# One 64x32 TensorE tile shape for attention scores and value products, and GpSimd copies of pairs of pairs

## The chip, the cores and the metric

The kernel runs on one core of one Trainium2 chip. The metric is the device time of one execution in microseconds; the number of a kernel is the median of its runs. TensorE is called PE, VectorE DVE, ScalarE ACT, GpSimd POOL, and SyncE, which starts most transfers, SP.

## What is computed

Two independent layers over 2048 positions of width 640, put side by side in the output (bf16):

```python
def _A_ref(x, Lambda_re, Lambda_im, B_re, B_im, C_re, C_im, log_dt, Dskip):
    dt = jnp.exp(log_dt)
    Lam_bar = jnp.exp(dt * Lam)                       # complex, one per state
    Bu = jnp.einsum("bld,pd->blp", x + 0j, B_bar)
    for t in range(L):
        h = Lam_bar[None, :] * h + Bu[:, t, :]
    y = 2.0 * jnp.einsum("blp,dp->bld", hseq, Cmat).real + x * Dskip[None, None, :]

def _B_ref(x, wq, wk, wv, wo):                        # 32 heads of 20, one key and one value head
    q = (x @ wq) ...                                  # [32 heads, 2048, 20]
    k = x @ wk
    v = x @ wv
    scores = jnp.einsum("bhqd,bkd->bhqk", q, k) * (Dh ** -0.5)
    p = _softmax(scores, axis=-1)
    return jnp.einsum("bhqk,bkd->bhqd", p, v) ... @ wo
```

A is a state-space layer, B an attention whose 32 heads share keys and values.

## The kernel before

**Attention, block by block.** A block is 512 queries of four heads; there are 4 x 8 = 32 of them. In each block the scores are made in 64 tiles of 128 keys by 512 queries of one head, so 2048 tiles in all (`NTILE`). A score tile is one product (`score`, L1616 to L1630): 32 rows of `KT` (20 of the head, one for a bias) by 128 keys as weights, 512 queries of `QT` moving. It fills a 32-row strip of the array (`tile_position=(32 * j, 0)`), and up to four of them, from four strips, run in one pass, each into a PSUM bank of its own.

**Two ways to the weights of the softmax.** Most tiles go through ACT: one exp of two or three banks (`fill`, L1530) into the ring `PR` of 24 slots. The others, called D tiles, go through DVE: a "first" (`fill_d`, recorded at L867) turns scores into an int16 whose bits read as a bf16 power of two, and three copies of it, shifted by 32, 64 and 96, are added up with weights of their own by the value product, which smooths the coarse exponential. A copy is an integer addition: on POOL two tiles at a time (`pool_source`, `copy`, L1858: `int64_add`), otherwise on DVE (`copy_source`). D tiles live in single slots of the tile `BIG`.

**Value products.** `pv_source` gathers one ready entry for each of the four heads; a product (`pv_fn`, L1946) has 128 keys by 32 columns of `VP` (or of `VS`, the values scaled for a shifted copy) as weights and 512 columns of weights moving, in a column strip (`tile_position=(0, 32 * j)`). All four accumulate in one PSUM bank (`MB`). A tile of ACT needs one such product and a D tile four. At the end of a block the bank is copied to `pvsb` (L1925) and the sums go through DRAM for their reciprocals.

**The other work.** Query projections, the output projection, and the state-space layer ("units", the C*B products, the y products) are tasks. Each takes a PSUM bank and puts its products in as PE has time (`ride`), four 32-column strips at a time (L800). Pieces of them, 32 rows at a time, also ride in a score pass that has a row strip free (`board`, `piece`, L810).

**The order of the work** is made by a planner in the kernel's own file (`Schedule`): engines take the steps that are ready by priority, with costs and due times written in as numbers (`STAGES` and others), some of them changing with the number of tiles begun. A step of PE has a mode, "S" for score passes and "C" for column strips, and changing it costs 97 ns in the plan. `port=True` marks steps of DVE and POOL which the plan never puts side by side. The order that comes out is emitted as one in-order instruction stream for each engine, with waits on semaphores (`Emitter`).

**PSUM** has eight banks: two groups of three for scores (`slots`), one for the value products, one for tasks (`misc`). The third bank of a group holds a third exp tile or a D tile of that pass.

Of the kernel before, what the change touches and what calls it, by code (L numbers as in the profile page):

```python
# [12 lines left out]
ALU = mybir.AluOpType  # L13
# [11 lines left out]
class Op:  # L25
# [3 lines left out]
                 "seq", "land", "dma_key", "idx", "tail", "mode", "load", "late", "port", "after", "due", "table", "psum", "twice", "rider", "fence", "lands", "clear")  # L29

    def __init__(self, eng, fns, dur, deps=(), prio=5, reads=(), writes=(), prev=None, gate=None, hook=None,
# [8 lines left out]
        self.twice = self.rider = None  # L40
# [6 lines left out]
class Schedule:  # L47
# [5 lines left out]
    ENGINES = ("pe", "act", "dve", "pool", "sp")  # L53
    OUT = {"pe": 200.0, "act": 130.0, "dve": 110.0, "pool": 150.0, "dma": 60.0}
    OWN = {"pe": 0.0, "act": 60.0, "dve": 115.0, "pool": 100.0}
# [3 lines left out]
    SLACK = {"pe": 60.0, "dve": 150.0}  # L59
# [50 lines left out]
    def seen(self, op, eng):  # L110

        if op.dma_key is not None:
            return op.end + self.OUT["dma"]
        if op.eng == eng:
            return op.end + self.OWN[eng] if eng in self.OWN else op.end
        return op.end + self.OUT[op.eng]

# [19 lines left out]
    def begin(self, op, eng):  # L137
# [5 lines left out]
        if eng == "pe":  # L143
            if op.mode != self.mode:
                op.dur += self.SWITCH
                self.mode = op.mode
            self.loads.append((self.t, op.load))
        if op.port:
# [25 lines left out]

    def pick(self, eng):
        urgent = None
        t = self.t
        cands = self.pending[eng]
# [26 lines left out]
        for op in can:  # L205
            p, dur = op.prio, op.dur
# [56 lines left out]
class Emitter:  # L263
# [9 lines left out]
    def plan(self):  # L273
        count = {e: 0 for e in Schedule.ENGINES}
        know = {e: {} for e in Schedule.ENGINES}
        snap = {}
# [4 lines left out]
        self.first = set()  # L281
        self.streams = {e: [] for e in Schedule.ENGINES}
        for op in self.order:
# [3 lines left out]
            def dep(o, key=None):  # L287
# [3 lines left out]
                if src == e and (e == "pe"):  # L291
                    return
                at = o.idx - 0.5 if key is not None and o.twice is not None and key != o.rider else o.idx
# [40 lines left out]
            for src, at, o in w:  # L334
# [4 lines left out]
                if at < o.idx:  # L339
                    self.first.add((id(op), id(o)))  # L340
# [17 lines left out]
        for e in ("pe", "act", "dve", "pool"):  # L358
            v = 0
            for op in self.streams[e]:  # L360
                if op.dma_key is None and id(op) in needed:
                    v += 1 if op.twice is None else 2
                    self.value[id(op)] = v
# [8 lines left out]
    def replay(self, rng):  # L372
# [3 lines left out]
        for op in self.order:  # L376
            e = op.eng
            t = free[e]
# [12 lines left out]
            else:  # L391
                end[id(op)] = t + op.dur + op.tail
                free[e] = t + op.dur - (S.EARLIER.get(e, 0.0) if op.psum else 0.0)
        return max(end.values())

    def emit(self, block):
        self.sems = {e: self.nc.alloc_semaphore(f"prog_{e}") for e in ("pe", "act", "dve", "pool")}
        self.dma_sems = {k: self.nc.alloc_semaphore(f"dma_{k}") for k in self.dma_keys}

        def run(e, be):  # L400
            for op in self.streams[e]:
                for o in self.waits_of[id(op)]:
                    if o.dma_key is not None:
                        be.wait_ge(self.dma_sems[o.dma_key], 16 * o.idx)
                    else:
                        be.wait_ge(self.sems[o.eng], self.value[id(o)] - ((id(op), id(o)) in self.first))
                ins = None
                for x, fn in enumerate(op.fns):
                    ins = fn(be)
                    if x == op.twice and id(op) in self.needed:  # L410
                        ins.then_inc(self.sems[e], 1)
                    if op.dma_key is not None:
                        ins.then_inc(self.dma_sems[op.dma_key], 16)
                if op.dma_key is None and id(op) in self.needed:
                    ins.then_inc(self.sems[e], 1)
# [23 lines left out]
class Ride:  # L439


    def __init__(self, bank, steps):
        self.bank, self.steps = bank, collections.deque(steps)
        self.open, self.last, self.end, self.rode = [], None, None, None
# [14 lines left out]
NQB, NKC, NGG = 4, 16, 8  # L459
NTILE = NQB * NGG * NKC * 4  # L460
# [7 lines left out]
class Build:  # L468
    CHUNKS = (3, 3)
    MISC = 1  # L470
    NPT = 24
    NOP = 7
    NRD = 3
    NDS = 20
    MORE = 21
# [71 lines left out]
    SPREAD = 18.658  # L547
    SEEDS, REPLAYS = (169732,), 12
# [28 lines left out]
    def quiet(self, order):  # L577
# [4 lines left out]
        for op in order:  # L582
            if op.eng == "pe":
# [3 lines left out]
        first = int(min(op.start for op in order if op.eng == "pe" and op.mode == "S") / step) - 20  # L587
        last = int(max(op.start for op in order if op.eng == "pe" and op.mode == "S") / step)
# [7 lines left out]
    def alloc(self, o):  # L596
# [27 lines left out]
        self.KT = sb(o, "KT", [128, S], BF16)  # L624
        self.VP = sb(o, "VP", [128, NKC, 32], BF16)
        self.VS = sb(o, "VS", [128, len(self.SHIFTS), NKC, 32], BF16)
# [6 lines left out]
        self.stg = sb(o, "stg", [128, 3, 512], BF16)  # L633
# [7 lines left out]
        self.lift = sb(o, "lift", [128, 4], FP32)  # L641
# [4 lines left out]
        self.dn = sb(o, "dn", [64, 2, 32], BF16)  # L646
        self.rc = sb(o, "rc", [64, 2, 32], BF16)
# [87 lines left out]
    GRAIN, KEEP_C = 256, 5  # L735

    def ride(self, bank, steps):

        p = self
        r = Ride(bank, [[list(m), list(deps), list(keys)] for m, deps, keys in steps])  # L740
        self.rides.append(r)

        def hook(op):
            mms, _, keys = r.steps[0]
            n = 0
            while mms and (not n or n + mms[0][2].shape[-1] <= p.GRAIN):
                out, lhsT, rhs = mms.pop(0)
                n += rhs.shape[-1]
                op.fns.append(p.product(r, out, lhsT, rhs, range(4), r.last is None))
                r.last = op  # L750
            op.reads = list(keys)
            if not mms:
                r.steps.popleft()
        while r.steps:
            mms, deps, keys = r.steps[0]
# [5 lines left out]
            op = self.pe([], self.mmt(n, k), deps=deps + (bank.last if r.last is None else []), prio=self.task_prio(), mode="C",  # L761
                         load=n, writes=[bank.key], hook=hook, gate=lambda: bool(r.steps))
            yield lambda: op.start is not None or not r.steps
            if op.start is None:
                self.s.pending["pe"].remove(op)
        while r.open:
            t0 = self.s.t
            self.s.at(t0 + self.PATIENCE)
            op = self.pe([], self.mmt(512), prio=1.5, mode="S", load=128.0, writes=[bank.key], hook=lambda op: self.alone(r, op),
                         gate=lambda: bool(r.open) and self.s.t >= t0 + self.PATIENCE - 1.0)  # L770
            yield lambda: op.start is not None or not r.open
            if op.start is None:
                self.s.pending["pe"].remove(op)
        self.rides.remove(r)
        return r.last

    PATIENCE = 2500.0

    def alone(self, r, op):

        step, left = r.open[0]
        x = min(left)
        left.remove(x)
        if not left:
            r.open.pop(0)
        op.fns = [self.piece(r, *m, x) for m in step[0]]
        op.reads = list(step[2])
        self.rode(r, op, x)
        self.n_alone += 1

    n_alone = 0

    def product(self, r, out, lhsT, rhs, cols, start):

        tag = object()
        r.end = tag
# [1876 lines left out]
```

## Time and profile before

| | us |
|---|---|
| runs: median (lowest to highest) of 3 | 697.88 (697.73 to 698.61) |
| profiled execution: span from first to last instruction | 695.9 |
| PE busy | 683.2 |
| ACT busy | 681.8 |
| DVE busy | 637.0 |
| POOL busy | 470.4 |

The profile's own time is its span; what lies around the span is in the runs only. The engine columns are the time in which at least one instruction of the engine was open. Products on PE are pipelined and their ends are modelled, so that a busy PE need not be at its peak; where the rhythm of PE matters, it is read from the starts of the products. `x` is a count of instructions; in the rows of groups, the number after the bar is busy time in all and the next the mean duration of one in ns, and behind the second bar stands the idle time of the engine just before them, with what ended it. In the rows of stretches the first pair is the stretch, then come the engines' busy times, the granted clock of PE as a share of the full one, the share of the DMA engines, and GB/s.

### The profile page before, as it was taken

To read this page: it belongs to the slowest core of one execution; us is meant where nothing else is said; L and a number is where in the kernel's file an instruction comes from. 1 tells how busy PE (TensorE), PEld (TensorE's weight loads), DVE (VectorE), ACT (ScalarE), POOL (GpSimd) and SP (SyncE) were. 2 spreads that over 40 slices of the span, in tenths; PEclk is the share of its full clock that TensorE was granted. 3 is DMA by queue.
4 is the path that set the end of the run, shared out by engine and by line. 5 is a ranking of instruction groups with operands and counts; after the bars stand their busy time and mean duration, and the time that the engine had idled before them with its cause. 6 is when DMAs were issued, how large, how long until landed. Compare 5 with 4: busy or idle time off the path is not lost.

```text
span 695.9 us, 27390 instructions
## 1 busy us (share of the span) xinstructions
PE 683.2 (98%) x11488; PEld 250.6 (36%) x11490; DVE 637.0 (92%) x1243; ACT 681.8 (98%) x703; POOL 470.4 (68%) x796
## 2 busy tenths in 40 slices
PE   8999999999999999999999999999999999999998
PEld 5322332334334333333433333334333332343335
DVE  7899999999999889999999999999999999977795
ACT  7999999999999999999999999999999999999996
POOL 4256666564587668767778777676776767788880
DMA  9659641211130111102110101131000001110001
GB/s 217 175 127 187 139 103 39 62 26 32 30 94 13 32 27 27 35 21 29 44 26 22 28 27 28 35 58 20 13 15 12 20 15 36 37 29 22 21 15 41
DMA packets 77591, 34.48 MB, mean 50 GB/s; under 512 B 58350, under 2 KB 77470, under 8 KB 77470
## 3 DMA queue, kind: packets, MB, share of 16 engines
q1 hardware_dynamic: 76650, 32.57, 20.3%
q8 instruction: 92, 1.51, 0.9%
q10 hardware_dynamic: 820, 0.16, 0.1%
q14 instruction: 29, 0.24, 0.1%
HBM read 11.53 MB, written 9.75 MB: 31 GB/s over the span
## 4 chain that ended last, share of the span: by engine, by line
PE 56%; ACT 42%; DVE 1%; issue 0%
ACT PR L1530 41%; PE MB L1946 21%; PE MB L800 14%; PE SC L1626 10%; PE MB L810 8%; PE MB L730 1%; DVE BIG L867 1%; PE SC L1162 1%; PE SC L726 1%; PE MB L726 0%; ACT L2197 0%; PE SC L730 0%; DVE pvsb L1925 0%; PE MB L1279 0%; DVE QT L867 0%
## 5 line engine op out<-in xcount | busy, mean ns | idle before, releaser
L1530 ACT ACTIVATE PR<-SC 128x1024 bf16<-128x1024 f32 (+1 forms) x678 | 666.6, 1131 | 4.5 <-PE SC L1626 3.3
L1858 POOL INT64_ADD BIG<-BIG x761 | 458.1, 617 | 198.1 <-DVE BIG L867 54.7
L867 DVE TENSOR_SCALAR BIG<-SC 128x512 int16<-128x512 f32 x560 | 376.2, 684 | 38.7 <-PE SC L1626 33.1
L1946 PE MATMUL MB<-BIG,VS 128*32 128x512 bf16 (+1 forms) x2468 | 269.8, 376 | 1.2 <-DVE pvsb L1925 0.9
L1626 PE MATMUL SC<-QT,KT 32*128 32x512 bf16 (+1 forms) x2073 | 265.3, 378 | 4.4 <-ACT PR L1530 1.8
L1946 PE MATMUL MB<-PR,VP 128*32 128x512 bf16 (+1 forms) x1495 | 222.3, 378 | 0.1
L1626 PEld LDWEIGHTS SC<-QT,KT 32*128 32x128 bf16 x2073 | 67.3, 91 | 133.8 <-ACT PR L1530 77.1
L1946 PEld LDWEIGHTS MB<-BIG,VS 128*32 128x32 bf16 x2468 | 68.5, 95 | 65.5 <-issue 41.4
L1946 PEld LDWEIGHTS MB<-PR,VP 128*32 128x32 bf16 x1495 | 55.1, 94 | 45.8 <-issue 33.0
L867 DVE TENSOR_SCALAR BIG<-BIG 128x1024 int16<-128x1024 int16 (+1 forms) x136 | 52.3, 419 | 0.9 <-PE MB L1946 0.4
L800 PE MATMUL MB<-CA,W 128*32 128x320 bf16 (+2 forms) x992 | 51.4, 299 | 0.4 <-DVE BIG L2366 0.4
L810 PE MATMUL MB<-xaT,BT 32*128 32x256 bf16 x192 | 37.1, 273 | 0.0
L800 PE MATMUL MB<-CT,W 128*32 128x512 bf16 (+1 forms) x640 | 36.0, 302 | 0.6 <-issue 0.6
L800 PE MATMUL MB<-xaT,BA 128*32 128x256 bf16 x800 | 31.8, 275 | 0.0
L810 PE MATMUL MB<-diagD,xaT 32*128 32x128 bf16 x320 | 31.3, 217 | 0.0
L810 PEld LDWEIGHTS MB<-diagD,xaT 32*128 32x128 bf16 x320 | 17.7, 92 | 29.1 <-ACT PR L1530 17.7
L800 PEld LDWEIGHTS MB<-CA,W 128*32 128x32 bf16 x992 | 22.8, 96 | 14.2 <-issue 5.7
L800 PE MATMUL MB<-xaT,BT 128*32 128x256 bf16 x608 | 26.2, 274 | 0.0
L2133 DVE CAST stg<-MB 128x512 bf16<-128x512 f32 x35 | 23.8, 680 | 1.8 <-PE MB L800 1.1
L862 DVE TENSOR_TENSOR prod<-MB,tab 128x1024 bf16<-128x1024 f32 x20 | 24.3, 1215 | 0.2
L867 DVE TENSOR_SCALAR BIG<-MB 128x512 int16<-128x512 f32 x35 | 23.8, 679 | 0.6 <-PE MB L1626 0.6
L2406 DVE TENSOR_TENSOR_SCAN g<-sc,hst,prod 128x256 bf16<-128x256 f32 x30 | 22.5, 749 | 0.0
(178 smaller groups left out, 502.4 us busy)
## 6 DMA issues: line engine op xcount, KB each, us to landing
out_dram<-stg SPq DMA_DIRECT2D x33, 128.0 KB, 2.0
qd<-BIG SPq DMA_DIRECT2D x20, 128.0 KB, 2.1
QT<-qd SPq DMA_DIRECT2D x28, 80.0 KB
OP<-pvsb SPq DMA_DIRECT2D x105, 20.0 KB
rdP<-recs SPq DMA_DIRECT2D x105, 20.0 KB
lbd<-BA SPq DMA_DIRECT2D x5, 320.0 KB, 2.7
CT<-in_B_x_dram SPq DMA_DIRECT2D x2, 640.0 KB, 5.3
BA<-in_A_B_re_dram SPq DMA_DIRECT2D x1, 800.0 KB, 7.5
```

The source lines that it names most:

```text
L726: r = e.matmul(out[32 * j:32 * j + 32], lhsT=lhsT[:, 32 * j:32 * j + 32], rhs=rhs, start=start, stop=stop, tile_position=(0, 32 * j), skip ...
L730: return lambda e: e.matmul(out, lhsT=lhsT, rhs=rhs, start=start, stop=stop, **kw)
L800: x = e.matmul(out[32 * j:32 * j + 32], lhsT=lhsT[:, 32 * j:32 * j + 32], rhs=rhs, start=start, stop=r.end is tag, tile_position=(0, 32 * ...
L810: return lambda e: e.matmul(out, lhsT=lhsT[at], rhs=rhs[at], start=start, stop=r.end is tag, tile_position=(32 * row, 0), skip_group_check ...
L862: return lambda e: e.tensor_tensor(out, a, b, op)
L867: return lambda e: e.tensor_scalar(out, a, s1, s2, op0=op0, op1=op1)
L1530: ex = self.act(lambda e: e.activation(dst, t[:, 0:512 * n], ACT.Exp, scale=1.0 / UNIT), 0.8333 * 512 * n + 64, table="exp", deps=[op], re ...
L1626: r = e.matmul(out[:, bank.off + lo:bank.off + lo + n], lhsT=p.KT[32 * j:32 * j + 32, 128 * c:128 * c + 128], rhs=p.QT[32 * j:32 * j + 32, ...
L1858: op.fns.append(lambda e: e.int64_add(words(dst), words(src), add))
L1946: r = e.matmul(bank.tensor[32 * j:32 * j + 32, bank.off + at:bank.off + at + n], lhsT=v[:, c, 0:32], rhs=rhs[:, lo:lo + n], start=first an ...
L2133: ev = self.dve(lambda e: e.tensor_copy(st, bank.ap), 645, deps=[prev], reads=[bank.key], writes=[key], prio=self.EV, gate=(lambda: last.e ...
L2406: o = self.dve(lambda e, ri=ri, init=init: e.tensor_tensor_scan(p.g[:, u, ri, :], rdec, p.prod[:, 1, 0, ri, :], init, ALU.mult, ALU.add), ...
```

## The change

**Scores.** A score tile now holds 64 keys by 512 queries for two heads, one in partitions 0 to 63 and one in 64 to 127. It takes four products of 64 rows by 32 columns, on one diagonal of the array's quadrants: rows 64 to 127 with columns 0 to 63, and rows 0 to 63 with columns 64 to 127 (`rows_at(1, j)`). The 64 rows hold two heads; `KT` is kept twice, each time with zeros in the rows of the other head. There are still 2048 tiles.

**Value products.** An entry is two products of 64 rows by 32 columns (`pv_add`), and two entries fill the other diagonal: rows and columns 0 to 63, rows and columns 64 to 127. D tiles need four entries as before.

**PE in the plan.** There are two lanes beside "pe", both in PE's one stream: "pt" for value products, "pb" for scores, each with half of the array. All of attention is one mode "U". The other work goes through both lanes, one lane after the other for each bank (`ride_source`); the rides in score passes (`board`, `piece`) are gone. A wait of one lane for a step of the other is a semaphore.

**D tiles.** They are taken singly by `d_source` whenever a bank is free, never as a part of a fill. The third banks of the two groups are shared by D tiles, tasks (`task_banks`) and third exp tiles. D tiles are held in pairs (`Pair`). POOL, or DVE, does copy 1 of a pair as one step of two tiles, and then copies 2 and 3 as one step of four tiles, which adds 64 to the first and to copy 1 (`step_of`, `CHAIN`). Copies by pairs need neighbouring slots.

**Sizes and numbers.** `PR` has 18 slots instead of 24; D slots 18 + 20 instead of 20 + 21; output staging 2 instead of 3; the cap on the share of D tiles (`SHARE`) 0.34 and 0.348 instead of 0.281 to 0.301. The first fill waits for the keys that it reads, not for all keys. The diagonal of the skip term of even rows is added into the C*B matrix once (`skip`) and leaves the y products. Reciprocals work on 128 x 16 instead of 64 x 32. There are new settings for the planner throughout, and functions to put state-space steps on POOL (`put`, `ON_POOL`), which the empty `ON_POOL` leaves unused.

The core of the diff:

```diff
-        self.KT = sb(o, "KT", [128, S], BF16)
-        self.VP = sb(o, "VP", [128, NKC, 32], BF16)
+        self.KT = sb(o, "KT", [128, 2, S], BF16)
+        self.VP = sb(o, "VP", [128, NHC, 32], BF16)
...
+    def rows_at(h, j):
+
+        t = h ^ j // 2
+        return slice(64 * t, 64 * t + 64), 64 * t
...
+    def ride_source(self, lane):
+
+        s = self.s
+        other = Schedule.HALVES[lane == "pt"]
+        for r in self.rides:
+            if not r.todo[lane] or r.on and lane not in r.on and r.todo[other]:
+                continue
+            o = r.on.get(other)
+            if o is not None and s.seen(o, lane) > s.t:
+                continue
...
-    def score(self, op, m, out, bank):
+    def scores(self, op, m, out, bank, deps=()):
...
-                r = e.matmul(out[:, bank.off + lo:bank.off + lo + n], lhsT=p.KT[32 * j:32 * j + 32, 128 * c:128 * c + 128],
-                             rhs=p.QT[32 * j:32 * j + 32, b % 12, at:at + n], start=True, stop=True, tile_position=(32 * j, 0))
+            for lo, c, q0, n in parts:
+                for j in range(4):
+                    at, row = self.rows_at(1, j)
+                    k = 64 * c + 32 * (j % 2)
+                    r = e.matmul(out[32 * j:32 * j + 32, bank.off + lo:bank.off + lo + n], lhsT=p.KT[at, x, k:k + 32],
+                                 rhs=p.QT[at, b % 12, q0:q0 + n], start=True, stop=True, tile_position=(row, 32 * j), skip_group_check=True)
...
+    def task_banks(self):
+
+        own = [b for b in self.free_banks if b in self.misc]
+        if not own and self.in_use < self.TASKS:
+            own = [b for b in self.free_banks if b in self.thirds]
+        return own
...
+    def step_of(self, d, free, eng):
+
+        s = self.s
+        if d.first is not None and len(d.todo) == 2 and len(d.tiles) == 2 and self.CHAIN:
+            if d.first[1].end is None or s.seen(d.first[1], eng) > s.t:
+                return None
+            if free > 1 and not self.short(d, 4):
+                return (2, 3)
+        if free < 1 or self.short(d, len(d.tiles)):
+            return None
+        return (d.todo[0],)
...
-        return Op("pool", [], self.POOL2, prio=1, port=True, hook=lambda op: self.copy(op, k, two, True))
-
-    POOL2 = 605.0
+        return Op("pool", [], self.POOL2 if len(ks) == 1 else self.POOL4, prio=1, port=True, hook=lambda op: self.copy(op, d, ks))
+
+    POOL2, POOL4 = 605.0, 1035.0
...
-    def pv_fn(self, b, j, v, kc, rhs, first, last):
+    def pv_add(self, op, b, j, entry, first, last):
...
+                for t in range(2):
+                    rows, to = slice(64 * t, 64 * t + 64), 32 * (2 * t + j)
+                    r = e.matmul(bank.tensor[to:to + 32, bank.off + at:bank.off + at + n], lhsT=v[rows, c, 0:32], rhs=rhs[rows, lo:lo + n],
+                                 start=first and not i, stop=last and i == len(parts) - 1, tile_position=(64 * t, to), skip_group_check=True)
```

More of the change, by code (lines that the diff above doesn't have):

```diff
@@ L733, in quads, with ride @@
         return self.QUADS and self.started
[L735 to L740, printed above, removed]
+    GRAIN = 256
+    def ride(self, bank, steps, cols=range(4)):
+        r = Ride(bank, steps, cols)
         self.rides.append(r)
[L743 to L755, printed above, removed]
+        yield lambda: not any(r.todo.values())
+        self.rides.remove(r)
+        return r.last
+    def ride_source(self, lane):
[7 more added lines that the diff above has]
+                continue
+            if r.last is None and any(o.end is None or s.seen(o, lane) > s.t for o in r.bank.last):
+                continue
+            mms, deps, keys = r.todo[lane][0]
+            if any(o.end is None or s.seen(o, lane) > s.t for o in deps):
+                continue
             n, k = 0, 0
@@ L774, in ride @@
[L774 to L796, printed above, removed]
+            return Op(lane, [], max(self.mmt(n, k), 32.0 * k), deps=list(r.bank.last) if r.last is None else (), mode="U", load=n / 2.0,
+                      prio=self.TASK2 if lane == "pt" else self.task_prio(), reads=keys, writes=[r.bank.key],
+                      hook=lambda op, r=r, k=k: self.ride_step(op, r, k))
@@ L1799, in copy_source @@
[L1799 to L1807 removed]
+        d, ks = can[0]
+        closing = d.b == self.pv_b and self.pv_filled[self.pv_b] == self.pv_need[self.pv_b]
```

905 lines of the change are left out of this document (454 added, 451 removed).

## The prediction

> **What bounds the kernel now.** I read the page's head first, then busy time by stretch, then groups by shape, then the waits and pieces of the timeline.
>
> ```profile
> span 695.9 us, 27390 instructions
> PE 683.2 (98%) x11488; PEld 250.6 (36%) x11490; DVE 637.0 (92%) x1243; ACT 681.8 (98%) x703; POOL 470.4 (68%) x796
> ```
> ```profile
> core 0: us, PE busy (x) PEld busy (x) DVE busy (x) ACT busy (x) POOL busy (x), PEclk, DMA share, GB/s
> 0.00:100.00 100.00, 96.49 (x1220) 34.31 (x1226) 91.18 (x234) 94.61 (x104) 54.34 (x105) 1.00 0.73 163
> 100.00:660.00 560.00, 554.35 (x9521) 200.31 (x9519) 518.93 (x956) 557.73 (x569) 399.45 (x664) 1.00 0.13 31
> 660.00:696.00 36.00, 32.34 (x755) 16.02 (x751) 26.92 (x55) 29.47 (x32) 16.61 (x28) 1.00 0.10 27
> ...
> 400.00:600.00 200.00, 197.17 (x3247) 68.38 (x3243) 194.02 (x362) 199.23 (x207) 145.09 (x244) 1.00 0.11 26
> ```
>
> Three engines look full; the clock is granted whole (1.00). ACT is truly full: 557.7 of 560 us in the middle. DVE has 518.9 of 560 there (92.7%), but 97.0% in the stretch 400 to 600. POOL has room.
>
> ```profile
> 18.41 1.02 ACT L1530 ACTIVATE PR<-SC 128x1024 bf16<-128x1024 f32 x1 [1.81 <-PE SC L1626]
> 682.14 5.54 ACT L1530 ACTIVATE PR<-SC 128x1024 bf16<-128x1024 f32 x5 [0.39 <-PE SC L1626]
> ```
> ```profile
> L1530 ACT ACTIVATE PR<-SC 128x1024 bf16<-128x1024 f32 (+1 forms) x678 | 666.6, 1131 | 4.5 <-PE SC L1626 3.3 <-PE MB L1626 0.3 <-PE MB L1946 0.2
> L867 DVE TENSOR_SCALAR BIG<-BIG 128x1024 int16<-128x1024 int16 (+1 forms) x136 | 52.3, 419 | 0.9 <-PE MB L1946 0.4
> ```
> ```profile
> L1530 ACT ACTIVATE PR<-SC 128x1024 bf16<-128x1024 f32 x579 | 544.7, 1068 | 4.3 <-PE SC L1626 3.3 <-PE MB L1626 0.3 <-PE MB L1946 0.2
> L1858 POOL INT64_ADD BIG<-BIG x761 | 458.1, 617 | 198.1 <-DVE BIG L867 54.7 <-PE MB L1946 22.1 <-DVE g L2406 19.3
> L867 DVE TENSOR_SCALAR BIG<-SC 128x512 int16<-128x512 f32 x560 | 376.2, 684 | 38.7 <-PE SC L1626 33.1
> L1530 ACT ACTIVATE PR<-SC 128x1536 bf16<-128x1536 f32 x98 | 141.6, 1505 | 0.1
> L867 DVE TENSOR_SCALAR BIG<-MB 128x512 int16<-128x512 f32 x35 | 23.8, 679 | 0.6 <-PE MB L1626 0.6
> ```
>
> So the work is 2048 score tiles of 128x512, each turned into weights either by ACT's exp or by DVE (a "first", then three shifted copies). DVE's are 560 + 35 = 595. The other 1453 are ACT's, 666.6 / 1453 = 0.459 us each. Exps begin at 18.41 and end at 682.14 + 5.54 = 687.7. So the span is 666.6 us of exps plus 29.3 of start, gaps and tail: **the span falls by 0.459 us for every tile that DVE takes from ACT.** A first costs DVE (376.2 + 23.8) / 595 = 0.672 us. DVE's copies are 52.3 us; everything else on DVE is 637.0 - 400.0 - 52.3 = 184.7. What keeps DVE from taking more is in its waits: 38.7 us before firsts, 33.1 of them for the score product on PE. Why it waits shows late in the kernel and in PE's rhythm:
>
> ```profile
> 626.32 0.69 DVE L867 TENSOR_SCALAR BIG<-SC 128x512 int16<-128x512 f32 x1 [0.18 <-PE SC L1626]
> 627.19 0.69 DVE L867 TENSOR_SCALAR BIG<-SC 128x512 int16<-128x512 f32 x1 [0.18 <-PE SC L1626]
> ```
> ```profile
> 300.33 0.38 PE L810 MATMUL MB<-BIG,xaT 32*128 32x512 bf16 x1
> 300.34 0.39 PE L1626 MATMUL SC<-QT,KT 32*128 32x512 bf16 x3
> 300.66 0.40 PE L1946 MATMUL MB<-BIG,VS 128*32 128x512 bf16 x4
> 300.88 0.38 PE L1946 MATMUL MB<-PR,VP 128*32 128x512 bf16 x1
> ...
> 301.21 0.39 PE L810 MATMUL MB<-BIG,xaT 32*128 32x512 bf16 x1
> ```
>
> Two groups of the same shape start 0.22 us apart (300.66, 300.88). Where the tile shape changes it is 0.33 (300.33 to 300.66, 300.88 to 301.21): 0.11 us is lost at each change, and scores come once per pass, here every 0.88 us. DVE then gets one first per pass and idles 0.18.
>
> **The change part by part.**
>
> *PE.* Sums of each product line over the span: value products, then score products, then the projections and state-space work in four column tiles, then their pieces that rode in score passes.
>
> ```profile
> 0.00:696.00 696.00, 296.26 (x3963) 76.93 (x3963) 1.00 0.21 50
> ...
> 0.00:696.00 696.00, 267.12 (x2112) 68.12 (x2112) 1.00 0.21 50
> ...
> 0.00:696.00 696.00, 192.85 (x4108) 80.83 (x4108) 1.00 0.21 50
> ...
> 0.00:696.00 696.00, 125.11 (x692) 42.98 (x692) 1.00 0.21 50
> ```
> ```profile
> L800 PE MATMUL MB<-CA,W 128*32 128x320 bf16 (+2 forms) x992 | 51.4, 299 | 0.4 <-DVE BIG L2366 0.4
> ```
>
> Before: (2112 + 692) / 4 = 701 score passes at 0.33 + 0.11 = 0.44 make 308 us; 3963 / 4 = 991 value groups at 0.22 make 218; 4108 / 4 = 1027 other groups at about 0.13 (a product of about 0.295, of which 0.165 is the tail that a 0.385 product shows over its 0.22 spacing) make 134. That is 660 of the 669 us between the first and the last exp: PE is the reason for the rhythm.
> After: no change of shape in attention, but every tile fills half of the array. The score half carries 2048 tiles x 0.22 = 451 us; the value half, with D tiles on DVE, (2048 + 3D) / 2 pairs: for D = 640 1984 x 0.22 = 436. The other work no longer rides for nothing; both halves carry it in full, 134 + 692 / 4 x 0.11 = 153 us each. The fuller half needs 604 us, 56 less than before, if the two run side by side. Nothing in the trace shows two such halves together. From above: one after the other they need 604 + 589 = 1193 us; from below, nothing is lost. I take little lost, since the four column tiles in the rows above run together with four different moving operands.
> The stream doubles: eight products per 0.22 us, one each 27 ns.
>
> ```profile
> 231.55 1.19 PE L800 MATMUL MB<-WO,OP 128*32 128x128 bf16 x72
> ```
>
> Here 72 products with their weight loads take 1.19 us, 0.165 of it tail: 14 ns each. So issue costs nothing. The Trainium skill ("TensorE: Matmul & The Clock Gate", section "Wait — 56ns, not 53.3ns?") gives about 62 ns per product where hardware decode is off; by that figure eight would take 0.50 us in place of 0.22 and PE would bind far above the time of before. This trace, with 14 ns, does not bear that out.
>
> *POOL.* A copy of two tiles is 458.1 / 761 = 0.602 us. The change does the first copy of a pair of tiles so, and the other two in one step of four tiles.
>
> ```profile
> L2215 POOL INT64_ADD fr<-fr x5 | 1.9, 399 | 2.6 <-DVE fr L867 2.6
> ```
>
> That one has half the width: 399 against 617 ns, so a doubling beyond it adds 0.436 and the step of four takes 0.602 + 0.436 = 1.04 (bounds: 0.60, if all were fixed cost; 1.20, if none). A pair costs 1.64 in place of 1.81; 320 pairs 525 us, beside 458 now. POOL's free time is 696 - 470 = 226, but it also stands back for DVE (54.7 us of its idle time ended with a DVE step on BIG), so I let DVE keep 20 us of copies, between 5 and today's 52.
>
> *DVE.* Two more key evictions, wider value scaling, narrower reciprocals: 184.7 becomes about 187. The firsts can now be fed singly at any moment, not once per pass. So its busy share in the middle should leave 92.7% and near the 97.0% of its best 200 us; I take 96%.
>
> *Start and tail.* Keys are evicted twice, two more on ACT and two on DVE. ACT idles 1.81 us before the first exp, so this costs 0 to 1.5 us; I take 0.5. The state-space and skip changes move a few products; nothing.
>
> *The sum.* Span T = 29.8 + 0.459 x (2048 - D). DVE's busy time is 91.2 + 26.9 at the ends and 0.96 x (T - 136) between; D = (that - 187 - 20) / 0.672. Both hold at D = 640: DVE 636.5, T = 29.8 + 646.2 = **676.0**. Runs take 697.88 (median) against this execution's 695.9, 2.0 around the span: **678 us.** With DVE at 97% and 5 us of copies T is 668; at 92.7% and 20 us, 684. So this case's own range is 670 to 686. PE's fuller half is then busy 604 of 649 us, 93%.
>
> **The rivals.**
>
> *The copies and the banks hold DVE back (0.12).* For: POOL would work some 500 us and also stand back; score tiles of DVE and the other work share three PSUM banks, and that work, done by halves in turn, keeps a bank about twice as long. Then D stays near 600: 29.8 + 0.459 x 1448 = 694, and runs of 690 to 700. Against: POOL's 226 free us, and firsts are no longer tied to passes.
>
> *One queue for two halves (0.13; slower).* Both halves are issued in one order. A product that waits for its data holds the other half behind it, scores and so ACT included; also, each piece of other work now hands over from one half to the other with a wait of PE for itself.
>
> ```profile
> PEld MB L1946 <- POOL BIG L1858: 10.2, 45, 0.3
> ```
>
> Such a wait is 10.2 / 45 = 0.23 us. From 669 - 604 = 65 us of them on, some 283 waits, nothing is gained; 960 pairs of value products will hang on copies. With 350 waits: 27 + 604 + 80 = 711, runs of 713. Said otherwise: 1193 - 669 = 524 us of the lesser half's 589, 89%, must run beside the other. Against: 45 waits now.
>
> *Two row tiles in one PSUM bank (0.02; slower).* In the passes above each of the four row tiles has a bank to itself; the change lets two row tiles write the same bank in other partitions. If they took turns, each product group would take 0.44: 901 + 306 + 27 = 1234. The Trainium skill ("TensorEngine Tiling (Array Packing)", section "Gotcha 1: PSUM Pressure") says different row tiles cannot access the same bank at once; no run here shows it. Against: the column tiles of the value products share a bank at full rate.
>
> *Better fed still (0.03).* DVE at 98% and hardly a copy: below 664.
>
> **How the numbers follow.** Measurement of this kernel can tell about 0.2%. The forecast has 0.70. Faster: 0.70, 0.03, and 0.07 of the copies' case; the same: its 0.04 between 696.5 and 699.3; slower: its last 0.01, 0.13 and 0.02. So 0.80, 0.04, 0.16. The range takes in the copies' case and stops short of the two slow ones: 664 to 702, about 0.18 outside.
>
> **What would show it.** Right: about 640 firsts and 1408 tiles in exps; DVE near 96% in the middle; no score pass, products of both kinds starting 0.22 us apart in each half; POOL's wide step near 1.04 us; ACT still full. Wrong: ACT with idle time before exps and releasers on PE (one queue); firsts near 600 with POOL full or banks scarce (copies); product groups 0.44 apart (banks).

## The result, and the profile after

| | before | after |
|---|---|---|
| runs, median (lowest to highest) of 4 | 697.81 (697.35 to 698.61) | 848.18 (844.0 to 851.13) |
| profiled execution: span | 695.9 | 842.3 |

The ratio is 1.2153 with an interval of 1.2112 to 1.2195: slower by 22%, where 3% faster was forecast. From the page of the kernel after, the lines that answer to those of before:

```profile
span 842.3 us, 58442 instructions
...
PE 744.3 (88%) x27181; PEld 445.2 (53%) x27181; DVE 633.5 (75%) x1162; ACT 697.6 (83%) x736; POOL 489.8 (58%) x622
...
q8 instruction: 212, 3.47, 1.7%
...
PE 81%; issue 11%; ACT 6%; DVE 1%; POOL 1%; DVEq 0%; ACTq 0%; POOLq 0%
...
L1516 ACT ACTIVATE PR<-SC 128x1024 bf16<-128x1024 f32 (+2 forms) x709 | 680.9, 1045 | 114.3 <-PE SC L1601 107.9
L1846 POOL INT64_ADD BIG<-BIG x586 | 477.3, 824 | 289.3 <-PE MB L1942 77.4
...
L852 DVE TENSOR_SCALAR BIG<-SC 128x512 int16<-128x512 f32 x474 | 318.2, 685 | 92.0 <-PE SC L1601 88.1
```

No engine is full any more. ACT idles 114 us before exps and DVE 92 before firsts, both for score products. So PE is late; yet PE is busy only 88% of the span. The chain has a part that it lacked before: 11% "issue", time in which PE waited for nothing that the profile shows. One line that the prediction does not mention has moved as well: queue 8, which carries instructions. The page of the kernel before has

```profile
q8 instruction: 92, 1.51, 0.9%
```

Its packets have 3.47 MB / 212 = 16 KB. PE's 27,181 products and as many weight loads are 54,416 instructions in the trace, with some that are neither; divided by 212 packets that is 256 instructions to a packet. Queue 8 brings PE its program, and there is 2.3 times as much of it.

The stretches of the kernel after (columns as before):

```profile
core 0: us, PE busy (x) PEld busy (x) DVE busy (x) ACT busy (x) POOL busy (x), PEclk, DMA share, GB/s
20.00:60.00 40.00, 25.84 (x1236) 16.58 (x1243) 13.74 (x53) 15.78 (x16) 2.63 (x5) 0.74 0.33 63
100.00:200.00 100.00, 95.22 (x2981) 47.20 (x2976) 88.84 (x158) 95.84 (x99) 69.89 (x87) 1.00 0.33 79
300.00:400.00 100.00, 88.55 (x3540) 59.11 (x3539) 77.01 (x131) 86.34 (x91) 66.75 (x83) 1.00 0.12 31
...
800.00:843.00 43.00, 29.45 (x1312) 20.05 (x1312) 9.07 (x20) 9.11 (x11) 0.00 (x0) 1.00 0.12 34
```

The loss sits in the start (ACT 15.8 of 40 us) and in the middle, where most stretches with more products lose more (ACT 86.3 of 100 us with 3540 products, 95.8 with 2981). The tail after the last exp is long as well; the tenth experiment comes back to it. The waits (engine, line, releaser: us in total, times, longest):

```profile
ACT PR L1516 <- PE SC L1601: 107.9, 109, 11.2
DVE BIG L852 <- PE SC L1601: 88.1, 165, 2.7
...
PEld SC L1601 <- issue: 32.6, 35, 2.2
...
PEld MB L1942 <- issue: 31.4, 41, 1.7
PEld SC L837 <- issue: 30.5, 40, 2.9
```

PE's loads stand still for up to 2.9 us with no releaser, on every line alike. A wait of one half for the other would have named a step.

**Where it stands still.** Two pieces of PE's timeline (start, us, engine, line, operation, count, idle time before). First a stretch that flows, then some of the rows with idle time:

```profile
301.60 0.40 PE L1601 MATMUL SC<-QT,KT 64*32 64x512 bf16 x4
301.61 0.40 PE L1942 MATMUL MB<-BIG,VS 64*32 64x512 bf16 x4
301.82 0.39 PE L1601 MATMUL SC<-QT,KT 64*32 64x512 bf16 x4
301.84 0.39 PE L1942 MATMUL MB<-PR,VP 64*32 64x512 bf16 x4
```
```profile
372.06 0.29 PE L837 MATMUL MB<-xaT,BA 64*32 64x256 bf16 x3 [0.62 <-issue]
...
375.53 0.23 PE L837 MATMUL SC<-BIG,xaT 64*32 64x128 bf16 x3 [1.50 <-issue]
...
379.00 0.29 PE L837 MATMUL MB<-xaT,BA 64*32 64x256 bf16 x3 [1.25 <-issue]
...
382.47 0.23 PE L837 MATMUL SC<-CA,W 64*32 64x128 bf16 x3 [1.70 <-issue]
```

The first shows that the new shape does what was hoped: scores and value products run side by side, a group of each every 0.22 us. The second shows the loss: four stops, each 3.47 us after the one before, though different products lie between them. Numbering PE's instructions in the trace, 89 of the 102 gaps over 0.2 us (81.0 of 92.7 us) stand at the same place modulo 256, where one packet of queue 8 ends and the next begins. A block is here what lies between two such places, and a stop is an end where the next instruction starts over 0.4 us after the one before it. Of 212 ends 106 are stops. A block that ends in a stop takes a median of 3.75 us, at least 3.18: 14.6 ns an instruction at the median. The trace shows how the time goes by: the next packet's transfer begins a median of 1.12 us after PE has entered a block, takes 1.1, and its instructions run 1.45 us after it lands, 3.67 in all. Why the transfer does not begin earlier no run shows. The median of all 212 blocks is 3.75 us too, and 212 blocks at 3.75 us are 795 of the 838 us between PE's first product and its last. In the kernel before the median block lasts 7.86 us, and two of 92 end in a stop.

The theory is then: **PE is fed 256 instructions in about 3.5 us (3.75 at the median here); the change asks for 16 instructions every 0.216 us, 13.5 ns each, and wherever products are shorter than 512 columns for more.** The rivals that stayed: the prediction's one queue for two halves (waits between them); a cost of each product on the array; something in the quadrants.

### The profile page after: what moved, and what is told of

It is laid out like the page before. It is cut to its first block, busy times and chain, and to the rows that moved or that the text cites. A ratio compares the mean times of both kernels' runs of the same rounds, so it can differ in the third digit from the quotient of the medians.

```text
span 842.3 us, 58442 instructions
## 1 busy us (share of the span) xinstructions
PE 744.3 (88%) x27181; PEld 445.2 (53%) x27181; DVE 633.5 (75%) x1162; ACT 697.6 (83%) x736; POOL 489.8 (58%) x622
## 3 DMA queue, kind: packets, MB, share of 16 engines
q8 instruction: 212, 3.47, 1.7%
## 4 chain that ended last, share of the span: by engine, by line
PE 81%; issue 11%; ACT 6%; DVE 1%; POOL 1%; DVEq 0%; ACTq 0%; POOLq 0%
PE SC L1601 28%; PE MB L1942 24%; PE SC L837 12%; PE MB L837 11%; ACT PR L1516 5%; PE MB L1601 2%; PE SC L1159 1%; POOL BIG L1846 1%; PE MB L770 0%; PE SC L766 0%; PE MB L766 0%; PE SC L1226 0%; DVE BIG L852 0%; PE SC L770 0%; PE MB L1286 0%
## 5 line engine op out<-in xcount | busy, mean ns | idle before, releaser
L1516 ACT ACTIVATE PR<-SC 128x1024 bf16<-128x1024 f32 (+2 forms) x709 | 680.9, 1045 | 114.3 <-PE SC L1601 107.9
L1601 PE MATMUL SC<-QT,KT 64*32 64x512 bf16 (+1 forms) x7900 | 556.0, 373 | 22.4 <-issue 19.1
L1942 PE MATMUL MB<-BIG,VS 64*32 64x512 bf16 (+1 forms) x5024 | 414.0, 371 | 12.2 <-issue 10.4
L852 DVE TENSOR_SCALAR BIG<-SC 128x512 int16<-128x512 f32 x474 | 318.2, 685 | 92.0 <-PE SC L1601 88.1
L1942 PE MATMUL MB<-PR,VP 64*32 64x512 bf16 (+1 forms) x2968 | 314.2, 374 | 11.0 <-issue 8.6
L1601 PEld LDWEIGHTS SC<-QT,KT 64*32 64x32 bf16 x7900 | 182.8, 91 | 137.1 <-ACT PR L1516 46.1
L1942 PEld LDWEIGHTS MB<-BIG,VS 64*32 64x32 bf16 x5024 | 150.0, 91 | 62.3 <-issue 20.1
L1942 PEld LDWEIGHTS MB<-PR,VP 64*32 64x32 bf16 x2968 | 99.7, 91 | 42.8 <-ACT PR L1516 17.4
L852 DVE TENSOR_SCALAR BIG<-MB 128x512 int16<-128x512 f32 x135 | 92.6, 686 | 27.1 <-PE MB L1601 25.1
L837 PE MATMUL SC<-CA,W 64*32 64x512 bf16 (+2 forms) x1120 | 61.7, 326 | 1.8 <-issue 1.7
L2131 DVE CAST stg<-MB 128x512 bf16<-128x512 f32 x19 | 12.9, 680 | 26.3 <-PE MB L837 26.0
```

The costliest lines, as they stand in the source:

```text
L837: x = e.matmul(out[32 * j:32 * j + 32], lhsT=w, rhs=rhs[at], start=start, stop=stop() if callable(stop) else stop, tile_position=(row, 32 ...
L852: return lambda e: e.tensor_scalar(out, a, s1, s2, op0=op0, op1=op1)
L1516: ex = self.act(lambda e: e.activation(dst, t[:, 0:512 * n], ACT.Exp, scale=1.0 / UNIT), 0.8333 * 512 * n + 50, table="exp", deps=w.ops, r ...
L1601: r = e.matmul(out[32 * j:32 * j + 32, bank.off + lo:bank.off + lo + n], lhsT=p.KT[at, x, k:k + 32], rhs=p.QT[at, b % 12, q0:q0 + n], star ...
L1942: r = e.matmul(bank.tensor[to:to + 32, bank.off + at:bank.off + at + n], lhsT=v[rows, c, 0:32], rhs=rhs[rows, lo:lo + n], start=first and ...
L2131: ev = self.dve(lambda e: e.tensor_copy(st, bank.ap), 645, deps=[prev], reads=[bank.key], writes=[key], prio=self.EV, gate=(lambda: last.e ...
```

## The experiments

**1 and 2. Fewer products.** The kernel after, with every second product of a group left out; the products that stay still stream 512 columns, so a group takes as long on the array.

```diff
-                for j in range(4):
+                for j in (0, 2):
...
-                for t in range(2):
+                for t in range(2 if first else 1):
```

The second run has the first of the two edits alone. Expected of both:

> The changed kernel with half of its products left out: each score tile makes two of its four products (half of the keys of each head), and each pair of value entries two of its four (all four only at the start of a block). Plan, waits, lanes, order and the 512 columns of each group stay as they are; products fall from 27181 to about 19060. Theory (delivery): PE's instructions come in blocks of 256 and the changed kernel's PE cannot get a block in less than some 3.4 to 3.75 us; 54400 instructions, 212 blocks, make 720 to 800 us. With 149 blocks that is 506 to 558 us, off the path, so the time falls to what the plan gives with 1439 tiles in exps: 690 to 715 us. Rival (one queue): a product that waits for its data holds the other half of the array; the waits are all still there, so 820 to 850. Rival (halves do not run side by side): groups still take their 512 columns, 820 to 850.

Of scores alone:

> The changed kernel with two of the four products of each score tile left out (half of the keys), nothing else. Products fall to about 22960, 179 blocks. Theory (delivery): 610 to 673 us for the blocks plus the start, in bursts still above what PE would need: 715 to 770 us, between the changed kernel and the one with both halves left out. Rivals (one queue, halves in turn): 820 to 850.

Measured, in one run each: 767.6 us with 149 packets, and 783.6 with 179. Both are far below 848 and below the 820 of the rivals, in the direction of delivery, and both are above its numbers. In the first the start was still late (ACT 16.76 of 40 us from 20 to 60), and the other work still came in bursts of short products with stops at block ends (24 of them; 39 in the second). Runs 6, 7 and 10 follow that up.

**3 and 4. The kernel before with more instructions.** Score and value products cut into two of 256 columns, or four of 128; shapes, order and array time as before, nothing left out.

```diff
+    CUT = 2
...
+    def pieces(self, parts):
+
+        w = 512 // self.CUT
+        return [(lo + x, c, at + x, w) for lo, c, at, n in parts for x in range(0, n, w)]
```

Two:

> The kernel before with each score and value product of 512 columns cut into two of 256, interleaved so that the strips run side by side as before; nothing is left out. Products rise from 11488 to about 17560, 137 blocks. Theory (delivery): 467 to 515 us for the blocks, so still hidden on the whole: 698 to 712. A rival in which every instruction costs its share (about 150 us for 15700 products more, from the difference of the two kernels) gives 698 + 58 = 756. One queue or halves in turn say nothing here: 698.

Four:

> The kernel before with each score and value product cut into four of 128 columns; nothing is left out, no tile shape, lane or wait of the change is in it. Products rise to about 29710, 232 blocks. Theory (delivery): 232 blocks at 3.4 to 3.75 us make 789 to 870 us, so 800 to 880. Rival (one queue) and rival (halves in turn): the kernel has neither, 698 to 710. Cost in proportion to instructions: 698 + 174 = 872, which e3 tells apart.

Measured: 706.84 us (ratio 1.0126, interval 1.0102 to 1.0149) in two, as delivery had it; 916.9 in four (one run), above its 800 to 880. The packets, and of the second the waits:

```profile
q8 instruction: 136, 2.23, 1.3%
```
```profile
q8 instruction: 228, 3.74, 1.8%
```
```profile
DVE BIG L867 <- PE SC L1626: 181.9, 246, 3.7
ACT PR L1531 <- PE SC L1626: 168.1, 187, 2.8
...
PEld MB L1950 <- issue: 117.4, 116, 3.0
```

50% more products cost 1.3%; two and a half times as many cost 31.5%, with the picture of the kernel after: 171 of 228 block ends are stops, a block in them 3.88 us. There are no halves and no 64x32 here, so neither is needed for the loss; and a fixed cost of each product would have shown in the first (that rival had 756 us). It is a limit that one either stays under or not.

**5. Products alone.** TensorE with nothing beside it:

> Leaves out the whole computation: TensorE alone runs seven sections, one after the other, and nothing else runs beside it: 60 products 128x128 of 512 columns; 160 groups of four 128x32 of 512; 320 groups of eight 64x32 (both diagonals) of 512, then of 256, then of 64 columns; 160 groups of four 64x64 (both diagonals) of 512; 160 groups of two 64x64 on one diagonal and four 64x32 on the other, of 512. Delivery of instructions as a limit of TensorE by itself (a fixed time for each block of 256, 3.4 to 3.75 us in the changed kernel): the groups of eight start 0.21 to 0.24 us apart at 512, at 256 and at 64 columns alike, since sixteen instructions take that long to come; the sections with four products or fewer go at 0.216 us. Rival, fetches are slow only because they share the DMA engines with the kernel's data: the blocks come in 2.6 us or less here, and the groups of 256 and of 64 columns start 0.16 us apart or less. Rival, no such limit: 0.11 us at 256 columns. Mixed section: 0.22 us a group if the two shapes can stand side by side, 0.3 us or more if each change of shape empties the array (0.11 us lost at each in the kernel before).

The timeline where 512 columns give way to 256, and 256 to 64:

```profile
98.42 28.76 PE L51 MATMUL PS<-X 64*32 64x512 bf16 x1024 [0.35 <-issue]
127.43 1.94 PE L51 MATMUL PS<-X 64*32 64x256 bf16 x128 [0.24 <-issue]
130.88 1.94 PE L51 MATMUL PS<-X 64*32 64x256 bf16 x128 [1.51 <-issue]
134.61 1.94 PE L51 MATMUL PS<-X 64*32 64x256 bf16 x128 [1.79 <-issue]
...
198.70 1.21 PE L51 MATMUL PS<-X 64*32 64x64 bf16 x128 [1.70 <-issue]
202.16 1.24 PE L51 MATMUL PS<-X 64*32 64x64 bf16 x128 [2.24 <-issue]
205.89 1.27 PE L51 MATMUL PS<-X 64*32 64x64 bf16 x128 [2.49 <-issue]
```

128 products, one block, and a stop; the next block comes 3.45 to 4.0 us after the last, whether its products have 256 columns or 64. From the first to the last start of a section, a group of eight takes 0.229 us at 512 columns, 0.219 at 256 and 0.232 at 64; within a block, at 256, it takes 0.109. So the limit holds with TensorE alone and hardly any data moving (the rival of shared DMA engines, 2.6 us or less, falls), and eight products of 512 columns, the scheme of the change, are already just over it. The granted clock was 0.50 in most of the section of 64 columns (from 203 to 270 us); its 0.232 us may owe a little to that, the 0.219 at 256 columns, at the full clock, does not. At the full clock four 128x32 or four 64x64 products take 0.216 a group, without stops. In the last section, 64x64 on one diagonal and 64x32 on the other, a pair of groups takes 0.66 us, 0.33 for each: they do not stand side by side at all.

**6 and 7. The start.** The 960 small products that make V (20 columns each) given in wider tiles, 480 of them, in the same order of work; alone, and together with the first experiment.

```diff
-            return lambda rows, j: p.xbT[rows, c, at + 32 * (j % 2):at + 32 * (j % 2) + 32]
+            return Keys(lambda rows: p.xbT[rows, c, at:at + 64])
...
-                bank.tensor[32 * j:32 * j + 32, bank.off + 32 * i:bank.off + 32 * i + 20], lhsT=lhs(c, 64 * (8 * tb + i))(slice(0, 128), j),
-                rhs=p.wvr[:, c, :], start=c == 0, stop=c == NC - 1, tile_position=(0, 32 * j), skip_group_check=True)
+                bank.tensor[64 * g:64 * g + 64, bank.off + 32 * i:bank.off + 32 * i + 20], lhsT=p.xbT[:, c, 64 * (8 * tb + i):64 * (8 * tb + i) + 64],
+                rhs=p.wvr[:, c, :], start=c == 0, stop=c == NC - 1, tile_position=(0, 64 * g), skip_group_check=True)
```

Alone:

> The changed kernel, its order of work untouched, with the small products that make V out of x given in wider shapes (two 128x64 for four 128x32, two 64x64 for four 64x32 in a half): 480 products of 20 columns fewer, 960 instructions of 54,416, nearly all before 60 us. Nothing is left out. Delivery theory: about four blocks of 256 fewer at 3.75 us, in a stretch where TensorE waits at block ends: 15 us less than the changed kernel, 826 to 838 us, and the first exp earlier than 29.9 us. Rival, the start is late through something else (the clock, the loads): 844 to 851 as before.

With half of the products:

> The same with half of the score products and half of the value products left out as in the first experiment (which took 767.6 us). Delivery theory: about 145 blocks of 256, the average far from binding, and the start as in the run above: 745 to 757 us. Rival, the start is late through something else: 765 to 770.

In the kernel after, PE's rows after 20 us, and the first exp:

```profile
21.44 1.05 PE L1226 MATMUL SC<-wvr,BIG 128*32 128x20 bf16 x108 [3.04 <-issue]
26.66 0.24 PE L1226 MATMUL SC<-wvr,BIG 128*32 128x20 bf16 x6 [4.17 <-issue]
```
```profile
29.90 1.94 ACT L1516 ACTIVATE PR<-SC 128x1024 bf16<-128x1024 f32 x2 [11.21 <-PE SC L1601]
```

In the sixth:

```profile
24.23 1.94 ACT L1529 ACTIVATE PR<-SC 128x1024 bf16<-128x1024 f32 x2 [5.54 <-PE SC L1614]
```

Measured: 836.8 us (ratio to before 1.1973, interval 1.1926 to 1.2019; the kernel after has 1.2153), within delivery's 826 to 838, the first exp 5.7 us earlier, and the granted clock from 20 to 60 us at 0.91 in place of 0.74. So the low clock of the start, which could have been a cause, followed for the most part from the starved PE. The seventh took 759.7, 8 us less than the first experiment, between delivery's 745 to 757 and the rival's 765 to 770.

**8. Fewer instructions with all the work.** Where two 64x32 products share rows and stand side by side, one 64x64 product: in scores and in the other work. The value products stay 64x32.

```diff
-                for j in range(4):
-                    at, row = self.rows_at(1, j)
+                for g in range(2):
+                    at, row = self.rows_at(1, 2 * g)
+                    r = e.matmul(out[64 * g:64 * g + 64, bank.off + lo:bank.off + lo + n], lhsT=p.KT[at, x, 64 * c:64 * c + 64],
```

> The changed kernel, its order of work untouched and nothing left out, with every pair of 64x32 products that share rows and stand side by side in columns given as one 64x64 product: scores two for four, the other work of the halves two for four, V as above; the value products stay 64x32. About 33,000 instructions for 54,416, some 128 blocks, about 5.5 us each on average. Delivery theory: the average no longer binds, only bursts of short products do; the planner's own end is 704 us and its kernel follows it to 712 to 735 us. Rival, 64x64 beside 64x32 empties the array at each change (0.11 us each, thousands of changes): above 800 us. Rival, the time went into the quadrants themselves (two row halves at once) and not into the count of instructions: 830 to 850.

Measured: 1513 us. Its busy line and a piece of PE's timeline:

```profile
PE 1502.0 (99%) x17811; PEld 558.1 (37%) x17813; DVE 647.1 (43%) x1162; ACT 737.4 (49%) x736; POOL 491.4 (33%) x622
```
```profile
299.77 0.40 PE L1619 MATMUL SC<-QT,KT 64*64 64x512 bf16 x2
300.10 0.40 PE L1960 MATMUL MB<-PR,VP 64*32 64x512 bf16 x4
300.43 0.62 PE L1619 MATMUL SC<-QT,KT 64*64 64x512 bf16 x4
300.98 0.40 PE L1960 MATMUL MB<-BIG,VS 64*32 64x512 bf16 x4
...
303.06 0.40 PE L1619 MATMUL SC<-QT,KT 64*64 64x512 bf16 x2
303.06 0.40 PE L850 MATMUL MB<-BIG 64*64 64x512 bf16 x2
```

The delivery theory's number, 712 to 735, was far off, and the rival of shapes was right: two groups of one shape start together (303.06), two of different shapes 0.33 us apart, one after the other, and PE is busy to the last. This says nothing against delivery, since the array binds long before; it says that the eight products per 0.22 us cannot be had in wider tiles while the value products are 32 columns wide.

**9. The other half of the change alone.** The kernel before with its shapes, and scored tiles in pairs with GpSimd's copies of pairs of pairs (`Pair`, `step_of`, `wide_at` and `copy` as in the change):

```diff
-        return len(self.d_free()) > taken + own + len(self.SHIFTS) - 1
+        return self.room(taken + own)
...
+    def room(self, n):
+
+        need = (n + 1 - (self.partner is not None) + 1) // 2
+        return not need or len(self.d_free()) > need
```

> The kernel before, its shapes of products kept, with the other half of the change alone: scored tiles held in pairs, GpSimd copying a pair or a pair of pairs, so that VectorE's copies fall from 136 to some 25. Nothing is left out. Theory of the prediction (in the kernel before TensorE had no room, so VectorE cannot be given more tiles by being freed of copies): the tiles of VectorE do not rise above 595 and the time is 700 to 712 us, not faster; the planner's own end is 703.7 us for 692.5 of the kernel before. Rival, VectorE's copies held it back: 40 us of VectorE freed, some 55 more tiles, 0.46 us of span each if all of it is used: 675 to 690.

Measured: 709.2 us (ratio 1.016, interval 1.0133 to 1.0186), as expected of a full PE. DVE's tiles are 556 + 29 = 585, and much of the 39 us that the copies left free went into waiting for scores, 61.4 us where it was 33.1:

```profile
L875 DVE TENSOR_SCALAR BIG<-SC 128x512 int16<-128x512 f32 x556 | 374.3, 685 | 69.8 <-PE SC L1634 61.4
```

How many tiles DVE takes is fixed in the plan, before anything runs, and the time follows the plan's 703.7 us. So the run is in line with a PE without room and does not prove it.

**10. Half of everything.** As the seventh, and of the other work's groups every second product left out too (`for j in cols[::2]`).

> The changed kernel, its order of work untouched, V in wide shapes, and half of all products left out: half of the score products, half of the value products (as in the seventh run) and half of the products of the other work of the two halves. About 98 blocks of 256 instructions for 212. Delivery theory: what the run with scores and values halved still lost against the planner's end of 704 us (759.7) came from bursts of other work; it goes, 706 to 725 us. Rival, the rest of the loss is something else than delivery (waits between the halves, the clock, loads): 745 to 760.

Measured: 730.0 us, between the two. Stops at block ends are all but gone: 2 of 108.

```profile
q8 instruction: 108, 1.77, 1.0%
...
L1529 ACT ACTIVATE PR<-SC 128x1024 bf16<-128x1024 f32 (+2 forms) x709 | 667.0, 1063 | 17.5 <-PE SC L1614 15.6
```
```profile
23.29 1.94 ACT L1529 ACTIVATE PR<-SC 128x1024 bf16<-128x1024 f32 x2 [4.60 <-PE SC L1614]
...
697.32 5.89 ACT L1529 ACTIVATE PR<-SC 128x1024 bf16<-128x1024 f32 x6 [0.29 <-PE SC L1614]
```

With the same order of work and the same array time as the kernel after, ACT's waits fall from 114.3 to 17.5 us and the time by 118 of the 150. Against the planner's own dates, exps are 14 us late by 57 us, 9 more evenly from there to the end, with no jumps; in the kernel after they are 134 us late by the last. The planner's end is 704 us, 12 above that of before. So 118 us are shown to go with the count of instructions, 12 lie in the order of work that the change made, and some 20 remain, most of them in the start, which no run took apart further. Seen on ACT, the 32 us by which this run is still slower than the kernel before are no longer exps: the first begins at 23.3 us for 18.4, gaps between them are 12.9 us for 2.7, and from the last one to the end it takes 23.3 us for 8.2. That tail is in the plan, which has 24.

## Why the prediction was wrong

**The step that failed** is "The stream doubles: eight products per 0.22 us, one each 27 ns. ... Here 72 products with their weight loads take 1.19 us, 0.165 of it tail: 14 ns each. So issue costs nothing." The term that it put at nothing is worth 118 us (tenth experiment). The 14 ns are true of a burst. 72 products are 144 instructions, less than the 256 that a packet brings; the row shows how fast PE runs what it already has, 7 ns an instruction. What comes after the packet it cannot show. In the fifth experiment the same PE does a group of eight in 0.109 us within a block and in 0.219 over many. The demand of the change is 13.5 ns an instruction without a pause, and the supply 13.7 to 14.5; what looked like a margin of a factor of two was a deficit of some per cent in attention, and of much more wherever products of 128 or 256 columns came in a row. The page had the warning: 92 packets of 16 KB, 256 instructions each, 696 / 92 = 7.6 us apart; with 2.3 times the instructions they would have to come 3.3 us apart, and whether they can is then the question.

The Trainium skill has this queue: "Runtime: NRT & Kernel Launch", section "Instruction fetch mechanics", gives blocks of 16 KiB, 256 instructions, fetched while the one before runs, at a cost "mostly hidden". The sizes agree with the trace; the cost does not, at this rate: half of the 212 crossings here were stops.

**The rest of the sum** was too low as well, and without the limit the change would still not have been faster: the tenth run takes 730 us. In T = 29.8 + 0.459 x (2048 - D) the 29.8 us around the exps were those of the kernel before and 0.5 more. They are 23.3 + 12.9 + 23.3 = 59.5 us in the tenth run, so this term was too low by 30. D was to be 640 and is 609, which adds 14. The exps themselves nearly fit: 667.0 us for the other 1439 tiles, 0.464 each for 0.459.

**The array's time** was right. Counted from the columns of the products in the trace, at 0.216 us for 512 (fifth experiment), score products are 442 us of one half, value products 419 of the other, other work 153 each: 595 in the fuller half, for 604 forecast, and the halves run side by side.

**Two row tiles in one bank** had 0.02, rightly: both kinds of groups put products of both row halves into one bank at 0.22 us. The rule of the Trainium skill weighed there ("TensorEngine Tiling (Array Packing)", section "Gotcha 1: PSUM Pressure") does not hold for these tiles, in different partitions of the bank: two turns of 0.22 would have made it 0.44.

**One queue for two halves** forecast the right direction, slower, and the right sign in the profile, ACT idle with PE as releaser, for the wrong reason; that it came out slower is luck for this rival. Its price was waits of the halves for each other; these would stay in the tenth experiment, whose order and semaphores are the same, and 118 us went. What such waits cost can only be a part of what remains.

**The figure of about 62 ns a product** that the prediction weighed, from the Trainium skill ("TensorE: Matmul & The Clock Gate", section "Wait — 56ns, not 53.3ns?"), stays not borne out: 27 to 29 ns a product were reached over thousands of them. It holds for hardware decode off, and no run shows which it was here. There was a limit on issue, of another size and kind.

**POOL's step** was 1.04 us forecast and 1.03 to 1.04 found in the two groups of wide steps. **DVE's copies** were to be 20 us and are about 15. **DVE's tiles** were to be 640 and are 609. That is the plan's number and not an effect of the starved PE: the tenth run has the same 609, with DVE busy 91% of the middle (510.55 of 560 us from 100 to 660) for the 96% forecast, and 73 to 89% in the kernel after. The rival of copies and banks had such a D; whether they are what kept the plan there is open. **The start** was to cost 0.5 us for keys; the first exp came 11.5 us later. V's 960 small products, of which the prediction says nothing, are a part of that: given as 480 they brought 5.7 us back. The rest was not taken apart.

**That the bound of the kernel before is PE's rhythm** is in line with the ninth experiment, where freeing 39 us of DVE gave no gain in time, but not proved by it, since the plan also gave DVE no more tiles.

## What to carry to other kernels

Before multiplying a tensor engine's instructions, divide: array time of a group by its instructions, loads included, against the rate at which the program itself comes in, here 256 instructions in 3.5 to 3.75 us. A burst in a trace gives the rate only if it is longer than one packet of the instruction queue; the queue's count of packets on the page, before and after, says at once whether to look. The end that the kernel's own planner gives is a second sign: 704 us for 692.5 says that by the planner's own costs the new order of work was slower. And a tile shape that lets many small products run together is bought with instructions: four 128x32 products fill the array for 8 instructions, eight 64x32 for 16.

## What the runs showed of the hardware

PE's program comes in packets of 256 instructions on a queue of its own; with nothing else running, blocks follow at 3.45 to 4.0 us however short the products (fifth run); a block that ends in a stop takes 3.75 at the median in the kernel after and 3.88 in the fourth run. 64x64 and 64x32 products on different diagonals do not overlap: each change of shape costs 0.11 us over the 0.22 of a group, 0.66 us for a pair of groups against 0.22; the Trainium skill ("TensorEngine Tiling (Array Packing)", section "Key Properties") says that a change of tiling mode drains the engine, and the trace agrees. A starved PE also loses its clock: 0.74 granted from 20 to 60 us in the kernel after (PE busy 25.8 of 40 us), 0.91 in the sixth run (36.6), 1.00 before (40.0).
